# GroupNorm on one core: an inner loop of four quarters, with register addresses, for VectorE's scaling

## Chip, cores, metric

One core of a Trainium2 (trn2) chip. The metric is device time in microseconds (us), the median of several executions. "Span" is the time from the first to the last instruction in the profile, a little under the device time.

## The reference

```python
def reference(x, g, b):            # x: 128 x 1024 x 32 x 16, bfloat16; 32 groups
    xr = x.reshape(B, G, C // G, H, W)
    mu = xr.mean(axis=(2, 3, 4), keepdims=True)
    var = ((xr - mu) ** 2).mean(axis=(2, 3, 4), keepdims=True)
    xn = (xr - mu) / jnp.sqrt(var + 1e-5)
    return xn.reshape(B, C, H, W) * g[None, :, None, None] + b[None, :, None, None]
```

The input is 134 MB and so is the output. Each must cross between HBM and SBUF once.

## The kernel before

The work is cut into 32 tiles of 4.19 MB (128 partitions x 16384 elements). Six slots of SBUF hold them, and a tile is scaled in place. For each tile, PE sums, VectorE makes the negative mean from the sum, ScalarE squares and sums (in two halves) and makes the standard deviation, and VectorE makes 32 pairs of scale and shift and applies them to 32 pieces of 512 columns.

SyncE issues all loads and stores, in this order. Note that loads 6 and 7 stand behind store 1 in its program, and load 6 can start only when store 0 has landed:

```python
for j in range(SLOTS):             # SLOTS = 6
    load(j)
for i in range(NT):                # NT = 32
    store(i)                       # waits for 4 increments of s_done per tile
    if i % RUN == RUN - 1:         # RUN = 2: stores in pairs, then loads in pairs
        first = i + 1 + SLOTS - RUN
        for j in range(first, min(first + RUN, NT)):
            load(j)                # waits until the slot's store has landed
```

VectorE, the engine that the change touches:

```python
def on_vector(e):
    e.addr_align(256, offset=128, max_nops=0)
    # ... memsets, the first mean ...
    with nc.Fori(0, NT, 1, engines=[e.engine]) as i:
        # ... mean of tile i+1; wait for ScalarE's result of tile i;
        #     reciprocal, scl (32 scales), bia (32 shifts), each with a drain ...
        for k in range(KC):                      # KC = 32, unrolled
            a = ring[:, bass.ds((i % SLOTS) * F + k * HW, HW)]
            e.tensor_scalar(
                out=a, in0=a, scalar1=scl[:, k : k + 1], scalar2=bia[:, k : k + 1],
                op0=ALU.mult, op1=ALU.add,
            )
            if k % (KC // NQ) == KC // NQ - 1:   # NQ = 4
                e.drain()
                e.sem_inc(s_done, 1)
```

Of the kernel before, what the change touches and what calls it, by code (L numbers as in the profile page):

```python
# [8 lines left out]
ALU = mybir.AluOpType  # L9
# [7 lines left out]
SLOTS = 6  # L17
# [3 lines left out]
NQ = 4  # L21
# [4 lines left out]
def kernel(  # L26
# [12 lines left out]
    nc = tc.nc  # L39
# [3 lines left out]
    HW = H * W  # L43
# [4 lines left out]
    KC = C // G  # L48
    F = KC * HW
# [9 lines left out]
    def sbuf(name, shape, dtype):  # L59
        return nc.alloc_sbuf_tensor(name, shape, dtype)  # L60


    ring = sbuf("ring", [P, SLOTS * F], BF16)
# [14 lines left out]
    scl = sbuf("scl", [P, KC], F32)  # L78
    bia = sbuf("bia", [P, KC], F32)
# [3 lines left out]
    def sem(name):  # L83
        return nc.alloc_semaphore(name)
# [6 lines left out]
    s_gbp, s_sum, s_mean, s_rstd, s_done = (  # L91
        sem("gbp"), sem("sum"), sem("mean"), sem("rstd"), sem("done"),
    )
# [110 lines left out]
                ).then_inc(s_rstd, 1)  # L204

    def on_vector(e):
        e.addr_align(256, offset=128, max_nops=0)
        e.memset(ones_b[:], 1.0)  # L208
        e.memset(eps_t[:], EPS)
        e.drain()  # L210
        e.sem_inc(s_ones, 1)
        e.wait_ge(s_gbp, 1)
        e.tensor_copy(out=gb[:], in_=gb_p[:])  # L213

        def mean(ps_i, nm_i):
            e.tensor_scalar(  # L216
                out=jd[:], in0=ps_i, scalar1=-inv_n, scalar2=None,
                op0=ALU.mult, op1=ALU.add, accum_out=nm_i,
            ).then_inc(s_mean, 1)

        e.wait_ge(s_sum, 1)
        mean(ps[:, 0:MM_FREE], nm[:, 0:1])
        e.drain()
        with nc.Fori(0, NT, 1, engines=[e.engine]) as i:
            e.wait_ge(s_sum, i + 2)
            mean(
                ps[:, bass.ds(((i + 1) % 2) * MM_FREE, MM_FREE)],
                nm[:, bass.ds((i + 1) % 2, 1)],
            )
            e.wait_ge(s_rstd, i + 1)  # L230
            e.drain()  # L231
            e.reciprocal(out=inv[:], in_=rstd[:, bass.ds(i % 2, 1)])  # L232
            e.drain()
            e.tensor_scalar(  # L234
                out=scl[:], in0=gb[:, 0:KC], scalar1=inv[:], scalar2=None, op0=ALU.mult
            )
            e.drain()
            e.scalar_tensor_tensor(  # L238
                out=bia[:], in0=scl[:], scalar=nm[:, bass.ds(i % 2, 1)],
                in1=gb[:, KC : 2 * KC], op0=ALU.mult, op1=ALU.add,  # L240
            )
            e.drain()
            for k in range(KC):
                a = ring[:, bass.ds((i % SLOTS) * F + k * HW, HW)]
                e.tensor_scalar(  # L245
                    out=a, in0=a, scalar1=scl[:, k : k + 1], scalar2=bia[:, k : k + 1],
                    op0=ALU.mult, op1=ALU.add,
                )
                if k % (KC // NQ) == KC // NQ - 1:
                    e.drain()  # L250
                    e.sem_inc(s_done, 1)

    with tc.tile_critical(no_gpsimd_drain=True):  # L253
        on_sync(nc.sync)
        on_gpsimd(nc.gpsimd)
        on_tensor(nc.tensor)
        on_scalar(nc.scalar)
        on_vector(nc.vector)
# [30 lines left out]
```

## Time and profile before

| | before |
|---|---|
| device time, median (range) of 3 | 636.95 us (636.89 to 637.66) |
| span of the profiled run | 635.3 us |
| load and store queue, share of 16 DMA engines | 98.7% |
| ScalarE busy | 481.1 us (76%) |
| VectorE busy | 386.8 us (61%) |

The DMA queue line of the page (queue, kind: packets, MB, share of the 16 engines' span), and one line of its costliest groups (line, engine, operation, count, then busy us, mean ns of one, then idle time before and what ended it):

```profile
q1 hardware_dynamic: 10368, 268.44, 98.7%
...
L245 DVE TENSOR_SCALAR ring<-ring,scl,bia x1024 | 342.3, 408 | 28.2 <-issue 28.2
```

The DMA engines are full. Nothing else is above 76%.

The timeline of VectorE for one tile of the opening, before (start, duration, engine, line, operation, count, idle time before):

```profile
53.08 0.69 DVE L216 TENSOR_SCALAR_CACHE_REDUCE jd<-ps 128x512 bf16 x1 [0.77 <-issue]
...
55.10 0.16 DVE L232 RECIPROCAL inv<-rstd 128x1 f32 x1 [1.32 <-ACT rstd L201]
...
56.22 2.68 DVE L245 TENSOR_SCALAR ring<-ring,scl,bia  x8 [0.23 <-issue]
59.11 2.67 DVE L245 TENSOR_SCALAR ring<-ring,scl,bia  x8 [0.21 <-issue]
62.00 2.67 DVE L245 TENSOR_SCALAR ring<-ring,scl,bia  x8 [0.21 <-issue]
64.89 2.67 DVE L245 TENSOR_SCALAR ring<-ring,scl,bia  x8 [0.21 <-issue]
68.31 0.69 DVE L216 TENSOR_SCALAR_CACHE_REDUCE jd<-ps 128x512 bf16 x1 [0.75 <-issue]
```

A scaling shows 408 ns, but eight of them take 2.67 us: one starts every 0.323 us, overlapping its neighbour. Between quarters 0.21 us pass (drain, one register instruction, dispatch).

The timeline of SyncE's DMA issues before (a row with x2 merges two issues, and its second column runs from the start of the first to the end of the second):

```profile
52.37 15.59 SPq L123 DMA_DIRECT2D out_dram<-ring  x2
73.54 10.05 SPq L115 DMA_DIRECT2D ring<-in_x_dram  x2
83.64 15.02 SPq L123 DMA_DIRECT2D out_dram<-ring  x2
...
240.88 0.91 SPq L123 DMA_DIRECT2D out_dram<-ring  x2
269.99 10.11 SPq L115 DMA_DIRECT2D ring<-in_x_dram  x2
280.14 0.91 SPq L123 DMA_DIRECT2D out_dram<-ring  x2
```

Two regimes are to be seen. In the opening (first three rows) the two stores of a pair lie 15 us apart: SyncE waits for VectorE, which ScalarE paces. Later the pair goes out in 0.91 us: both tiles were ready, SyncE waits only for landings, and VectorE has slack.

The table of windows for the same stretch before (window, length, busy us of PE, PEld, DVE, ACT, POOL, granted clock, DMA share, GB/s):

```profile
68.00:76.00 8.00, 6.55 (x23) 2.73 (x24) 5.45 (x18) 7.86 (x5) 0.00 (x0) 0.70 0.94 406
76.00:84.00 8.00, 2.15 (x10) 0.78 (x8) 6.82 (x21) 7.85 (x3) 0.00 (x0) 0.94 1.04 451
84.00:92.00 8.00, 0.00 (x0) 0.00 (x0) 6.00 (x20) 7.71 (x5) 0.00 (x0) 0.50 0.96 414
92.00:100.00 8.00, 6.70 (x24) 2.81 (x25) 6.53 (x20) 7.85 (x3) 0.00 (x0) 0.71 1.04 442
```

The last column: the view counts a packet whole in the window in which it starts. So the DMA share can pass 1, and one packet of 32 KB more or less on each of the 16 engines changes an 8 us window by 65 GB/s. With the queue never empty the column stays at 406 to 451 GB/s. With each packet's bytes spread over its own time, worked out from the trace, it is 431 to 433 GB/s in all four windows.

### The profile page before, as it was taken

Reading aid. Unit: us, or ns where it says so; the run is one execution under the profiler, and the core shown is the slowest. Engines: PE = TensorE matmul, PEld = TensorE weight load, DVE = VectorE, ACT = ScalarE, POOL = GpSimd, SP = SyncE. Lnnn points to the kernel's source line nnn. Section 1 sums busy time; section 2 is a strip of 40 time slices with the busy share of each in tenths; the row PEclk is TensorE's granted clock in tenths of the full one; section 3 lists DMA queues with packets and bytes.
Section 4 is the critical chain, followed back from the end, with each engine's and each line's share of the span. In section 5 each row is a group of like instructions: output and inputs, shape, how many; then the busy total and the mean of one; then the engine's idle time right before and its main releaser. Section 6 shows DMA issues by size and latency. Waiting matters only on the chain.

```text
span 635.3 us, 6588 instructions
## 1 busy us (share of the span) xinstructions
PE 254.8 (40%) x1025; PEld 107.0 (17%) x1025; DVE 386.8 (61%) x1189; ACT 481.1 (76%) x194; POOL 0.8 (0%) x6
## 2 busy tenths in 40 slices
PE   1976518054180632707327072360823608163000
PEld 0332203021030210303113031120301203021000
DVE  0047777777757276572766727567275772757760
ACT  0499999999979498593986939779397793979800
POOL 0000000000000000000000000000000000000000
PEclk9999769568595685957859577595775958778555
DMA  8999999999999999999999999999999999999994
GB/s 362 429 437 421 429 431 427 435 433 435 435 429 429 429 429 437 431 439 435 429 429 429 429 435 431 431 429 427 423 433 421 437 427 419 427 427 431 429 416 205
DMA packets 10466, 268.46 MB, mean 423 GB/s; under 512 B 1248, under 2 KB 1248, under 8 KB 1248
## 3 DMA queue, kind: packets, MB, share of 16 engines
q1 hardware_dynamic: 10368, 268.44, 98.7%
q10 hardware_dynamic: 96, 0.00, 0.0%
q14 instruction: 2, 0.02, 0.0%
HBM read 134.22 MB, written 134.22 MB: 423 GB/s over the span
## 4 chain that ended last, share of the span: by engine, by line
DMA 51%; ACT 28%; PE 9%; DVEq 3%; DVE 3%; issue 2%; ACTq 1%; SPq 0%; POOLq 0%
DMA out_dram<-ring 34%; ACT ja L187 27%; DMA ring<-in_x_dram 17%; PE ps L165 9%; DVE ring L245 2%; DVEq L250 2%; DVEq L245 1%; ACT var L197 1%; DVEq L231 0%; ACTq L196 0%; ACT rstd L201 0%; ACTq L187 0%; DVE bia L238 0%; DVE scl L234 0%; DVE jd L216 0%
## 5 line engine op out<-in xcount | busy, mean ns | idle before, releaser
L187 ACT ACTIVATE ja<-ring,nm 128x8192 fp8e5 x64 | 455.8, 7122 | 113.7 <-DVE jd L216 108.2
L165 PE MATMUL ps<-ring,eye 128*128 x1024 | 254.6, 412 | 311.9 <-POOLq L154 300.2
L245 DVE TENSOR_SCALAR ring<-ring,scl,bia x1024 | 342.3, 408 | 28.2 <-issue 28.2
L165 PEld LDWEIGHTS ps<-ring,eye 128*128 128x128 bf16 x1024 | 106.9, 104 | 459.2 <-issue 363.4
L216 DVE TENSOR_SCALAR_CACHE_REDUCE jd<-ps 128x512 bf16 (+1 forms) x33 | 22.8, 692 | 139.4 <-PE ps L165 124.3
L232 DVE RECIPROCAL inv<-rstd 128x1 f32 x32 | 5.2, 164 | 40.2 <-ACT rstd L201 37.6
L187 ACT ACTIVATION_READ_ACCUMULATOR ja<-ring,nm 128x1 f32 x64 | 11.9, 186 | 0.0
L197 ACT ACTIVATE var<-sq,eps_t 128x1 f32<-128x1 f32 x32 | 9.4, 294 | 2.2
L201 ACT ACTIVATE rstd<-sq,var 128x1 f32<-128x1 f32 x32 | 9.4, 294 | 2.2
L238 DVE SCALAR_TENSOR_TENSOR bia<-scl,nm,gb 128x32 f32<-128x32 f32 x32 | 8.1, 252 | 4.7
L234 DVE TENSOR_SCALAR scl<-gb,inv 128x32 f32<-128x32 f32 x32 | 7.7, 242 | 2.7
L213 DVE COPY gb<-gb_p 128x64 f32<-128x64 f32 x1 | 0.2, 225 | 10.2 <-PE gb_p L159 10.2
L159 PE MATMUL gb_p<-gb_b,rep 32*128 32x64 bf16 x1 | 0.2, 208 | 11.8 <-DMA gb_b<-in_b_dram 11.8
L216 DVE DVE_READ_ACCUMULATOR jd<-ps (+1 forms) x33 | 2.7, 83 | 0.0
L181 ACT ACT_TABLE_LOAD x1 | 1.3, 1283 | 1.9 <-issue 1.9
L159 PEld LDWEIGHTS gb_p<-gb_b,rep 32*128 32x128 bf16 x1 | 0.1, 98 | 11.7 <-issue 11.7
L208 DVE MEMSET ones_b<- 128x128 bf16 x1 | 0.2, 165 | 1.7 <-SPq L253 1.7
L144 POOL TENSOR_SCALAR_AFFINE_SELECT rep<-ones_b 32x128 bf16<-32x128 bf16 x1 | 0.3, 303 | 0.0
L140 POOL TENSOR_SCALAR_AFFINE_SELECT eye<-ones_b 128x128 bf16<-128x128 bf16 x1 | 0.3, 292 | 1.4 <-DVEq L210 1.4
L181 ACT ACTIVATE warm<-eps_t 128x1 f32<-128x1 f32 x1 | 0.2, 202 | 0.0
L273 POOL MEMSET const-bfloat16-1.0<- 128x1 bf16 x1 | 0.1, 101 | 0.0
L273 POOL MEMSET const-uint8-127<- 128x1 uint8 x1 | 0.1, 101 | 0.0
(3 smaller groups left out, 0.3 us busy)
## 6 DMA issues: line engine op xcount, KB each, us to landing
ring<-in_x_dram SPq DMA_DIRECT2D x30, 4096.0 KB, 19.5
out_dram<-ring SPq DMA_DIRECT2D x30, 4096.0 KB, 29.2
ring<-in_x_dram SPq DMA_DIRECT2D x4, 2048.0 KB, 17.0
out_dram<-ring SPq DMA_DIRECT2D x8, 1024.0 KB, 20.2
gb_b<-in_g_dram ACTq DMA_DIRECT2D x1, 2.0 KB, 7.0
gb_b<-in_b_dram ACTq DMA_DIRECT2D x1, 2.0 KB, 10.2
```

Source lines behind the costliest of these rows:

```text
L159: e.matmul(out=gb_p[:], lhsT=rep[:], rhs=gb_b[:], start=True, stop=True).then_inc(s_gbp, 1)
L165: last = e.matmul(out=ps[:, bass.ds((i % 2) * MM_FREE, MM_FREE)], lhsT=eye[:], rhs=ring[:, bass.ds((i % SLOTS) * F + k * MM_FREE, MM_FREE) ...
L181: e.activation(out=warm[:], in_=eps_t[:], func=ACT.Sqrt)
L187: e.activation(out=ja[:], in_=ring[:, bass.ds((i % SLOTS) * F + h * (F // 2), F // 2)], func=ACT.Square, bias=nm[:, par : par + 1], scale=1.0,
L197: e.activation(out=var[:], in_=sq[:, 0:1], func=ACT.Identity, bias=eps_t[:], scale=inv_n)
L201: e.activation(out=rstd[:, par : par + 1], in_=sq[:, 1:2], func=ACT.Sqrt, bias=var[:], scale=inv_n,).then_inc(s_rstd, 1)
L216: e.tensor_scalar(out=jd[:], in0=ps_i, scalar1=-inv_n, scalar2=None, op0=ALU.mult, op1=ALU.add, accum_out=nm_i,).then_inc(s_mean, 1)
L232: e.reciprocal(out=inv[:], in_=rstd[:, bass.ds(i % 2, 1)])
L234: e.tensor_scalar(out=scl[:], in0=gb[:, 0:KC], scalar1=inv[:], scalar2=None, op0=ALU.mult)
L238: e.scalar_tensor_tensor(out=bia[:], in0=scl[:], scalar=nm[:, bass.ds(i % 2, 1)], in1=gb[:, KC : 2 * KC], op0=ALU.mult, op1=ALU.add,)
L245: e.tensor_scalar(out=a, in0=a, scalar1=scl[:, k : k + 1], scalar2=bia[:, k : k + 1], op0=ALU.mult, op1=ALU.add,)
L250: e.drain()
```

## The change

Intent: make VectorE's loop so short that all of its program lies in the first block of instructions (in these traces instructions arrive in packets of 8 KB), so that no alignment is needed. A loop over quarters holds eight scalings; since the quarter is a register, the addresses of scale and shift must come from registers too.

```diff
     def on_vector(e):
-        e.addr_align(256, offset=128, max_nops=0)
 ...
-            for k in range(KC):
-                a = ring[:, bass.ds((i % SLOTS) * F + k * HW, HW)]
-                e.tensor_scalar(
-                    out=a, in0=a, scalar1=scl[:, k : k + 1], scalar2=bia[:, k : k + 1],
-                    op0=ALU.mult, op1=ALU.add,
-                )
-                if k % (KC // NQ) == KC // NQ - 1:
-                    e.drain()
-                    e.sem_inc(s_done, 1)
+            with nc.Fori(0, NQ, 1, engines=[e.engine]) as q:
+                for k in range(KC // NQ):
+                    c = q * (KC // NQ) + k
+                    a = ring[:, bass.ds((i % SLOTS) * F + c * HW, HW)]
+                    e.tensor_scalar(
+                        out=a, in0=a, scalar1=scl[:, bass.ds(c, 1)], scalar2=bia[:, bass.ds(c, 1)],
+                        op0=ALU.mult, op1=ALU.add,
+                    )
+                e.drain()
+                e.sem_inc(s_done, 1)
```

## The prediction

> **What bounds the kernel now.** The DMA engines. The page's DMA queue table gives the load/store queue 98.7% of the 16 engines' span, and the table of windows shows 420 to 450 GB/s in nearly every 10 us up to 626 us. Each tile costs 2 x 4.19 MB, 19.7 us. VectorE has slack: 386.8 us busy (61%). In the timeline one tile costs it about 14.3 us, of which four quarters of 2.67 us. In the steady state the second tile of a pair is finished at 313.0 us and SyncE issues its store at 319.5 us: 6.5 us of slack. The chain of waits names ScalarE (28%) and PE, but mostly in the shadow of a full DMA queue.
>
> **What the change does.**
> 1. It removes the alignment instruction. Today VectorE branches at 1.04 us and its first memset starts at 1.66 us; now near 1.1 us. Worth nothing: the first matmul over data waits for a load that lands at 14.1 us.
> 2. Each of the 1024 scalings (L245) gets two fused register instructions instead of one. The scalings follow each other every 0.323 us, while the sequencer, where it runs ahead, takes 0.130 us for each. I estimate 0.24 to 0.28 us with the second instruction and the longer first one (today's register instructions take 0.05 to 0.15 us), still under 0.323 us. So a quarter keeps its 2.67 us.
> 3. Each quarter's head becomes serial: increment 0.04, branch 0.056, restart about 0.14 (today's outer back edge shows these), register instructions 0.15 and 0.06, gaps. I estimate 0.7 us idle before a quarter instead of 0.21: +2.0 us per tile, 14.3 becoming 16.3 us. The Trainium skill (Runtime: NRT & Kernel Launch, instruction fetch mechanics) says that a taken branch to a target outside the two held pages stalls for a fetch. The new body is small, so I expect none; no run here shows one yet.
>
> **On the critical path.** In the steady state nothing: +2 us per tile fits in 6.5 us. Only the opening is tight. The six first loads and store 0 are 29.4 MB; by 68 us the trace has moved all but 1.1 MB, about 2.5 us of work, and store 1 is issued at 67.6 us. Tiles 0 and 1 together delay it by about 3 us, to 70.5 us, when the queue is nearly dry; load 6 waits for store 0. That leaves a hole of 1 to 2.5 us, which a saturated queue never recovers. Later stores of the opening slip by 4 to 6 us, but with 5 to 11 MB queued. The last store is issued at 613.8 us with a queue lasting to 626 us; 2 to 4 us later is covered.
>
> **Predicted time:** 638.5 us, 80% range 636.4 to 641.5. Faster by over 2%: 0.01; within 2%: 0.95; slower by over 2%: 0.04.
>
> **What would show it.** Step 2: scalings still 0.32 us apart, busy time near 342 us. Step 3: idle before the scalings rising from 28.2 us to 85 to 95 us, 128 inner branches, no more instruction packets. Opening: store 1 near 70.5 us and a dip in DMA between 69 and 73 us. Steady state: stores in pairs, 39.3 us apart, never waiting for VectorE.
>
> **What would make it wrong.** A sequencer cost above 0.323 us per scaling (register pointers dearer than estimated): several us per tile; beyond about 6 us the stores slip. A code layout in which the inner branch fetches each time: 128 stalls, clearly slower. If the queue still holds work at 70.5 us, the change is exactly nothing, 637 us.

## More of the kernel before

A tile that waits for nothing takes 14.15 us from mean to mean. In the opening it takes 15.2 to 15.5 us, because VectorE waits for ScalarE's result (1.32 us in the second row shown): there ScalarE sets the pace.

## The result, and the profile after

| | before | after |
|---|---|---|
| device time, median (range) of 4 | 637.3 us (636.89 to 637.66) | 640.83 us (639.44 to 641.19) |
| span of the profiled run | 635.3 us | 639.1 us |
| VectorE's tile, nothing waited for | 14.15 us | 16.58 us |

The ratio is 1.0052 (95% interval 1.0034 to 1.0069): within 2%, but clear of noise, and slower.

The same lines of the page, after:

```profile
q1 hardware_dynamic: 10368, 268.44, 98.5%
...
L246 DVE TENSOR_SCALAR ring<-ring,scl,bia x1024 | 351.0, 413 | 91.5 <-issue 91.5
```

The first memset comes 0.55 us earlier, for nothing. The idle time ahead of the scalings has grown by 63 us, of which none is put down to another engine: "issue" means that the profile shows nothing else to wait for, and the records put VectorE's own sequencer (the part that reads its instructions and computes addresses) at work there.

VectorE's timeline, the same tile after:

```profile
55.79 0.69 DVE L215 TENSOR_SCALAR_CACHE_REDUCE jd<-ps 128x512 bf16 x1 [0.91 <-issue]
...
56.74 0.16 DVE L231 RECIPROCAL inv<-rstd 128x1 f32 x1 [0.24 <-issue]
...
58.17 2.75 DVE L246 TENSOR_SCALAR ring<-ring,scl,bia  x8 [0.53 <-issue]
61.70 2.74 DVE L246 TENSOR_SCALAR ring<-ring,scl,bia  x8 [0.77 <-issue]
65.21 2.74 DVE L246 TENSOR_SCALAR ring<-ring,scl,bia  x8 [0.77 <-issue]
68.72 2.74 DVE L246 TENSOR_SCALAR ring<-ring,scl,bia  x8 [0.78 <-issue]
72.37 0.69 DVE L215 TENSOR_SCALAR_CACHE_REDUCE jd<-ps 128x512 bf16 x1 [0.91 <-issue]
```

A quarter's start is 0.77 us after the end of the one before (0.21 us before the change), and a quarter itself takes 2.74 instead of 2.67 us. Where the second number comes from is in the view of one source line, its register instructions first before, then after (duration ns min/median/max):

```profile
L245 DVEq FUSED_REGOPS  x1024: 57/57/123, 40.8 to 611.9; - x171
```
```profile
L246 DVEq FUSED_REGOPS  x1920: 46/75/179, 41.4 to 622.1; - x192
```

In the sequence of records a scaling is now preceded by one of 179 ns and one of 46 ns, and with dispatch and gaps the sequencer needs 0.332 us, just more than the 0.323 us of the engine. The engine now follows the sequencer.

SyncE's issues after, the rows that answer to those of before:

```profile
54.94 16.93 SPq L123 DMA_DIRECT2D out_dram<-ring  x2
72.37 11.60 SPq L115 DMA_DIRECT2D ring<-in_x_dram  x2
88.09 16.92 SPq L123 DMA_DIRECT2D out_dram<-ring  x2
...
243.12 0.91 SPq L123 DMA_DIRECT2D out_dram<-ring  x2
272.29 10.22 SPq L115 DMA_DIRECT2D ring<-in_x_dram  x2
282.56 0.91 SPq L123 DMA_DIRECT2D out_dram<-ring  x2
```

Store 0 goes out 2.6 us later than before, store 1 at 71.5 instead of 67.6 us, store 2 at 88.1 instead of 83.6 us. Later, pairs still go out in 0.91 us. And the windows after:

```profile
68.00:76.00 8.00, 2.49 (x6) 0.96 (x7) 5.35 (x17) 6.59 (x5) 0.00 (x0) 0.67 0.82 352
76.00:84.00 8.00, 6.56 (x27) 2.64 (x25) 6.46 (x20) 7.85 (x3) 0.00 (x0) 0.90 1.05 393
84.00:92.00 8.00, 0.00 (x0) 0.00 (x0) 5.30 (x17) 6.59 (x5) 0.00 (x0) 0.74 1.06 459
92.00:100.00 8.00, 6.09 (x19) 2.45 (x20) 6.46 (x20) 7.85 (x3) 0.00 (x0) 0.62 0.91 393
```

In these 32 us the DMA moves 12.8 MB instead of 13.7 MB (rates times 8 us). With the bytes spread over each packet's own time the four rates are 384, 378, 427 and 433 GB/s, so it is mainly the first two windows that lose, and they differ in kind. In the first, the 16 engines stand idle for 0.8 us in all: when store 1 is issued, 0.04 MB is left in the queue. In the second no engine is idle and about 4 MB or more are queued, but from 80 to 84 us packets of 32 KB that otherwise take 1.21 us take up to 2.3 us. The same happens from 100 to 104 us. Longer packets cost 1.6 us between 76 and 110 us, against 0.2 us before. Why they take longer no run shows.

Summing the packets of both traces in order of completion, the changed kernel is level with before to within 0.3 us at seven tiles' worth of data (72 us; a tile is 4.19 MB), and then late by 1.3 us at eight, 1.9 us at ten, and 2.7 us at sixteen (160 us). It falls no further behind until 470 us. By the end it is 3.7 us late. So most is lost in the opening, and the rest, about 1 us, after 470 us.

### The profile page after: what moved, and what is told of

It is laid out like the page before. It is cut to its first block, busy times and chain, and to the rows that moved or that the text cites. A ratio compares the mean times of both kernels' runs of the same rounds, so it can differ in the third digit from the quotient of the medians.

```text
span 639.1 us, 7899 instructions
## 1 busy us (share of the span) xinstructions
PE 263.2 (41%) x1025; PEld 109.3 (17%) x1025; DVE 395.5 (62%) x1189; ACT 482.1 (75%) x194; POOL 0.8 (0%) x6
## 4 chain that ended last, share of the span: by engine, by line
DMA 53%; DVE 18%; issue 10%; DVEq 9%; PE 4%; ACT 2%; SPq 1%; ACTq 0%; POOLq 0%
DMA out_dram<-ring 45%; DVE ring L246 16%; DMA ring<-in_x_dram 7%; PE ps L165 4%; DVEq L246 4%; DVEq L242 3%; ACT ja L187 2%; DVEq L230 1%; DVE bia L237 1%; DVE scl L233 1%; DVEq L215 0%; DVE inv L231 0%; DVE jd L215 0%; SPq L115 0%; DVEq L223 0%
## 5 line engine op out<-in xcount | busy, mean ns | idle before, releaser
L246 DVE TENSOR_SCALAR ring<-ring,scl,bia x1024 | 351.0, 413 | 91.5 <-issue 91.5
L165 PE MATMUL ps<-ring,eye 128*128 x1024 | 263.0, 422 | 307.7 <-POOLq L154 288.8
L165 PEld LDWEIGHTS ps<-ring,eye 128*128 128x128 bf16 x1024 | 109.2, 107 | 461.2 <-issue 369.9
L215 DVE TENSOR_SCALAR_CACHE_REDUCE jd<-ps 128x512 bf16 (+1 forms) x33 | 22.8, 692 | 100.5 <-PE ps L165 81.4
L215 DVE DVE_READ_ACCUMULATOR jd<-ps (+1 forms) x33 | 2.7, 83 | 0.0
```

The lines of the kernel that those rows point to most:

```text
L165: last = e.matmul(out=ps[:, bass.ds((i % 2) * MM_FREE, MM_FREE)], lhsT=eye[:], rhs=ring[:, bass.ds((i % SLOTS) * F + k * MM_FREE, MM_FREE) ...
L215: e.tensor_scalar(out=jd[:], in0=ps_i, scalar1=-inv_n, scalar2=None, op0=ALU.mult, op1=ALU.add, accum_out=nm_i,).then_inc(s_mean, 1)
L246: e.tensor_scalar(out=a, in0=a, scalar1=scl[:, bass.ds(c, 1)], scalar2=bia[:, bass.ds(c, 1)], op0=ALU.mult, op1=ALU.add,)
```

## The experiments

Theory A: VectorE's longer tile matters only in the opening, where it delays stores 1 and 2 until the queue has nothing left. Rivals: B, the place of the code in the instruction blocks; C, an equal loss for every looped tile; D, the slower VectorE, or its register traffic, slows the DMA or the chain in some other way; E, the loop costs something besides its time.

### 1 and 2: the alignment alone

```diff
 # e1_no_align, against the kernel before; e2_loop_align is the changed kernel with this line added
-        e.addr_align(256, offset=128, max_nops=0)
```

> The kernel before without its alignment instruction, nothing else. Theory A (the time is lost in the opening, because slower scaling delays stores 1 and 2 until the DMA queue runs dry): 637.3 us, within 0.5 us of before, since the scaling is untouched. Rival B (code layout: what matters is where the loop lies in the instruction blocks): clearly slower, with more instruction packets than the 2 of before, and a longer head of each tile on VectorE.

> The changed kernel with the alignment instruction put back. Theory A: 640.8 us as the changed kernel, within 0.7 us; first memset back at 1.66 us. Rival B (the loss of the alignment costs the 3.5 us): 637.3 us.

Measured on the same chip (before: 637.05 us): e1 637.13 us, ratio 1.0002 (0.9988 to 1.0015); e2 640.49 us, ratio 1.0057 (1.0043 to 1.0070). e1 has 2 instruction packets, like before. Rival B is out for the bulk of the loss: the line is worth nothing either way. Something small does hang on it. In the five runs of e2 the device time is 1.69 to 1.75 us above the span, as in before; in the four of the changed kernel it is 2.09 to 2.14 us. Some 0.4 us of the changed kernel's time therefore lies outside the span, and in its trace an instruction packet stands at 640.99 us, after the span has ended. The only other kernel with both signs is e7 below, which has the same VectorE program. That this packet is the cause is likely, not shown.

### 3 and 4: which tiles

```diff
-        with nc.Fori(0, NT, 1, engines=[e.engine]) as i:
+        for first, last, trips in [(0, 8, 0), (8, 32, 4)]:   # e3; e4: [(0, 8, 4), (8, 32, 0)]
+            with nc.Fori(first, last, 1, engines=[e.engine]) as i:
+                tile_of(i, trips)      # trips 0: the unrolled code of before
```

Both start with an alignment of their own (offset 16), meant to put both loops in one block. The traces do not quite bear that out: e3 has an instruction packet at 169 us and e4 one at 185 us, near the change of loops. The data of e3 are no later after it than before it.

> Tiles 0 to 7 scaled by the unrolled code of before, tiles 8 to 31 by the inner loop, both loops in one aligned block. Theory A: 637.3 to 638.0 us, no hole in the DMA between 70 and 90 us, although VectorE takes 16.6 us for each of 24 tiles. Rival C (every looped tile costs the same, wherever it stands, 3.5 us / 32): 639.9 us.

> The mirror: tiles 0 to 7 by the inner loop, tiles 8 to 31 unrolled. Theory A: 639.3 to 640.8 us, with the same two holes in the DMA near 71 and 84 us. Rival C: 638.2 us.

Measured (before: 637.05 us): e3 638.03 us, ratio 1.0020 (1.0006 to 1.0033); e4 640.32 us, ratio 1.0051 (1.0037 to 1.0064). The windows of e3:

```profile
68.00:76.00 8.00, 5.66 (x18) 2.31 (x19) 5.01 (x17) 7.86 (x5) 0.00 (x0) 0.61 0.96 414
76.00:84.00 8.00, 3.33 (x16) 1.30 (x14) 7.49 (x23) 7.85 (x3) 0.00 (x0) 1.00 1.06 459
```

No hole: 414 and 459 GB/s where the changed kernel had 352 and 393. Eight looped tiles at the beginning cost 3.3 us, 24 elsewhere cost 1.0 us. Rival C expected the opposite order. But e3 is slightly above Theory A's range, and its interval excludes zero: the looped tiles of the steady state are not free.

In e3 a looped tile took 17.48 us, not 16.58: the same inner branch was followed by about 0.25 us until the next instruction instead of 0.135 us. The only known difference is the place of the loop in the block. Even so e3 lost only 1.0 us.

### 5 and 6: the first three tiles

The same edit with `[(0, 3, 4), (3, 32, 0)]` for e5 and `[(0, 3, 0), (3, 32, 4)]` for e6.

> Inner loop for tiles 0 to 2 alone, the other 29 unrolled. Theory A (two holes, behind stores 0 and 1, because stores 1 and 2 come late): 638.6 to 640.3 us, with the loss already made by 90 us. Rival C (a share per looped tile): 637.4 us.

> The mirror: tiles 0 to 2 unrolled, 29 tiles by the inner loop. Theory A: 637.0 to 638.3 us, stores 1 and 2 issued near 68 and 84 us as before. Rival C: 640.2 us.

Measured (before on this chip: 636.57 us): e5 638.94 us, ratio 1.0031 (1.0019 to 1.0043); e6 637.93 us, ratio 1.0018 (1.0005 to 1.0031). Three looped tiles of 32 cost 2.4 us, the other 29 cost 1.4 us. The ratios less one add up (0.0031 + 0.0018 = 0.0049) to nearly the 0.0052 and 0.0057 of all tiles looped. In e5 the packets were 1.9 us late at eight tiles' worth of data and 3.4 us late at eleven (111 us, not by 90 us as expected). Then they no longer fell behind, and were 2.0 us late at the end; in e6 they were level to within 0.3 us until 314 us.

### 7 and 8: early stores, VectorE unchanged

```diff
     def store_parts(i):
-        return NQ if i >= NT - IN_PARTS else 1
+        return NQ if i >= NT - IN_PARTS or i < 3 else 1
 ...
-                e.wait_ge(st[j % SLOTS], 16 * (j // SLOTS))
+                e.wait_ge(st[j % SLOTS], 16 * sum(store_parts(t) for t in range(j % SLOTS, j, SLOTS)))
```

e7 is the changed kernel with this edit, e8 the kernel before with it.

> The changed kernel, all tiles by the inner loop, but the stores of tiles 0 to 2 in four parts, each issued when its quarter is scaled, so that the queue has work when the first loads end. Theory A: 636.5 to 638.0 us, the two holes gone though VectorE is as slow as in the changed kernel. Rival D (the slower VectorE itself, or its register traffic, slows the DMA or the chain): 640.8 us, no gain.

> The kernel before with the same early stores in parts. Theory A: the queue of before hardly ran dry, so at most 0.5 us of gain: 636.5 to 637.3 us.

Measured (before: 636.57 us): e7 639.67 us, ratio 1.0050 (1.0037 to 1.0063); e8 638.00 us, ratio 1.0021 (1.0008 to 1.0034). Both miss their ranges. Taken by the time alone, e7 speaks for rival D. The windows of e7 say otherwise:

```profile
68.00:76.00 8.00, 2.56 (x7) 0.97 (x8) 5.41 (x17) 6.59 (x5) 0.00 (x0) 0.64 1.01 425
76.00:84.00 8.00, 6.31 (x27) 2.58 (x25) 6.45 (x20) 7.85 (x3) 0.00 (x0) 0.93 1.05 448
84.00:92.00 8.00, 0.00 (x0) 0.00 (x0) 5.30 (x18) 6.59 (x5) 0.00 (x0) 0.71 1.02 438
92.00:100.00 8.00, 7.33 (x23) 2.94 (x24) 6.46 (x21) 7.85 (x3) 0.00 (x0) 0.65 1.03 442
```

The holes are gone although VectorE is just as slow (at ten tiles' worth of data e7 is level with before), and longer packets cost only 0.4 us between 76 and 110 us. What e7 gained there it paid elsewhere: its data are within 0.8 us of before until 350 us, those of e8 within 0.6 us, and both lose the rest after that. The control e8 shows that the early stores in parts themselves cost 1.4 us on a kernel whose queue had no hole; why was not found. By spans, medians of the runs: before 634.9, e8 636.3, e7 637.5 us. So with early stores the loop costs 1.2 us of span, the same size as the rest that e3 and e6 left (1.0 and 1.3 us by spans), and on top e7 has the 0.4 us outside the span. The sum fits; it is a sum made after the fact.

### 9: time without a loop

```diff
             for k in range(KC):
+                if k % (KC // NQ) == 0:
+                    for _ in range(3 if k < KC // 2 else 2):
+                        e.reciprocal(out=pad[:], in_=inv[:])   # 128 x 1, result unused
+                        e.drain()
```

Here `pad` is a new tile of 128 x 1, and the alignment is at offset 16.

> The unrolled kernel before, with ten tiny drained reciprocals per tile (three, three, two, two, ahead of its quarters) that stretch VectorE's tile from 14.15 to about 16.6 us, the time of a looped tile; no inner branch, no register addresses for scale and shift. Theory A (only VectorE's time per tile matters): 640.0 to 641.3 us, stores 1 and 2 near 71 and 88 us. Rival E (the inner loop itself costs something besides its time): below 639 us. In the steady state the second store of a pair should land on the last engine 9.88 us after the first, as with looped tiles, if time is all that matters, and 9.82 us, as before, if not.

Measured (before: 636.98 us): 641.96 us, ratio 1.0069 (1.0055 to 1.0083). The tile took 16.77 us, stores 1 and 2 went out at 73.3 and 90.1 us, and the scalings were those of before (408 ns each). No inner branch, no register address of scale or shift, and the loss is there, larger with a still later store 1. The windows:

```profile
68.00:76.00 8.00, 1.13 (x5) 0.41 (x4) 6.16 (x21) 6.38 (x5) 0.00 (x0) 0.70 0.72 307
76.00:84.00 8.00, 8.00 (x27) 3.04 (x25) 6.75 (x25) 7.85 (x3) 0.00 (x0) 0.66 1.00 393
```

A bare delay is enough: the engines stand idle for 2.5 us, and longer packets cost another 1.9 us by 110 us. So neither register traffic (rival D) nor the loop itself (rival E) is needed for the opening's loss, and in e7 both were present without it. The time lies 0.7 us above the expected range, with stores 1 and 2 about 2 us later than expected.

### 10, 11 and 12: the number of heads

```diff
-            with nc.Fori(0, NQ, 1, engines=[e.engine]) as q:
-                for k in range(KC // NQ):
-                    c = q * (KC // NQ) + k
+            per = KC // trips                       # trips 1, 2 or 8
+            with nc.Fori(0, trips, 1, engines=[e.engine]) as q:
+                for k in range(per):
+                    c = q * per + k
 ...
-                e.drain()
-                e.sem_inc(s_done, 1)
+                    if (k + 1) % min(per, KC // NQ) == 0:
+                        e.drain()
+                        e.sem_inc(s_done, 1)
```

With eight trips SyncE counts eighths. One and two trips have an alignment at offset 16.

> One trip of 32 scalings: register addresses for all, one loop head per tile instead of four. Tile about 15.4 us (16.6 less three heads of 0.4 us each). Theory A: 637.8 to 639.3 us, between before and the changed kernel, store 1 near 69.5 us. If the register addresses and not the heads made the loss: 640 us and more.

> Eight trips of four scalings, eight heads per tile: about 20.0 us per tile, more than the 19.7 us that the DMA engines need. VectorE becomes the bound: 40 us before the first scaling, 32 tiles of 20.0 us, and about 12 us for the last stores: 680 to 697 us, stores waiting for VectorE to the end. If the opening alone counted, whatever the tile time: 645 us.

> Two trips of sixteen scalings, addresses of scale and shift from registers as in the changed kernel (with one trip they had been folded into constants), two loop heads per tile instead of four. Tile about 15.8 us: 32 scalings at 0.332 us, two heads of 0.78 us, two drains inside a trip at about 0.39 us. Theory A: stores 1 and 2 near 70 and 86 us, and 638.2 to 640.0 us, between before and the changed kernel. If heads do not matter and register addresses alone do: 640.5 us and more. In the steady state the second store of a pair should land 9.88 us behind the first on the last engine if register addresses cause that, 9.82 to 9.85 us if the four heads do.

| kernel | trips | tile, us | store 1 issued, us | store 2 issued, us | median, us | ratio to before (95%) | MB queued at store 1 | engines idle between 70 and 80 us | lost to longer packets between 76 and 110 us |
|---|---|---|---|---|---|---|---|---|---|
| e10_trips1 | 1 | 14.38 | 68.2 | 84.4 | 637.28 | 1.0003 (0.9990 to 1.0017) | 1.53 | 0.0 us | 0.1 us |
| e12_trips2 | 2 | 15.87 | 70.3 | 86.2 | 638.94 | 1.0035 (1.0021 to 1.0048) | 0.63 | 0.0 us | 1.5 us |
| changed kernel | 4 | 16.58 | 71.5 | 88.1 | 640.83 | 1.0052 (1.0034 to 1.0069) | 0.04 | 0.8 us | 1.6 us |
| e9_delay_all | none | 16.77 | 73.3 | 90.1 | 641.96 | 1.0069 (1.0055 to 1.0083) | 0.03 | 2.5 us | 1.9 us |
| e11_trips8 | 8 | 19.99 | 77.4 | 97.4 | 684.99 | 1.0756 (1.0739 to 1.0772) | 0.00 | 6.9 us | 1.9 us |

e10 came out below its range, for a reason that the built program shows: with one trip the loop variable is known to be zero, so the addresses of scale and shift were folded back into constants and the scalings stayed at 408 ns. It tests one loop head, not register addresses, and one head is free: its tile of 14.38 us is still shorter than the 15.2 to 15.5 us that ScalarE allows in the opening. e12 does have register addresses (413 ns), and lies between, as Theory A expected. In these five the time rises with the moment of stores 1 and 2.

The last three columns, worked out from one trace of each kernel, correct Theory A on one point. In e12 the queue never ran dry and no engine stood idle, and yet its data were 1.6 us late at ten tiles' worth: all of it went into packets that took longer. e2 is the same (0.40 MB queued, no idle time, 1.8 us). e4 and e5 had 0.06 and 0.05 MB queued, 1.3 us of idle time and 1.8 us of longer packets. Where 1.2 MB or more were queued at store 1 (before 1.70, e1 2.07, e3 1.39, e6 1.24, e10 1.53) there was no idle time and at most 0.2 us of longer packets. So late stores cost time in two ways, and an empty queue is only one of them.

e11 shows the other end. VectorE's timeline there:

```profile
313.81 1.41 DVE L258 TENSOR_SCALAR ring<-ring,scl,bia  x4 [0.78 <-issue]
315.99 1.41 DVE L258 TENSOR_SCALAR ring<-ring,scl,bia  x4 [0.78 <-issue]
318.31 0.69 DVE L215 TENSOR_SCALAR_CACHE_REDUCE jd<-ps 128x512 bf16 x1 [0.91 <-issue]
```

Every 2.19 us a head of 0.78 us; no wait for another engine is left. The tile of 19.99 us exceeds the DMA's 19.7 us, VectorE bounds the kernel, and 48 us are lost. The step from 16.6 to 20.0 us costs more than ten times what the step from 14.15 to 16.6 us costs: that is where the slack ends.

### What stays open

Why packets take longer after late stores. And a rest of 1.0 to 1.4 us for looped tiles after the opening (e3, e6). SyncE's pairs of stores give a hint. Between 320 and 440 us a pair follows the last after 39.30 to 39.33 us in before, e4 and e5 (steady state unrolled), and after 39.38 to 39.45 us in the changed kernel, e2, e3, e6, e7 and e12 (steady state looped).

The expectations of e9 and e12 had set a test for its cause: how long after the first store of a pair the second one lands. In that stretch it is 9.81 to 9.83 us in before. e9, with long tiles and constant addresses, has 9.84 to 9.87 us (pairs 39.33 to 39.35 us apart), nearer to before. e12, with register addresses and two heads, has 9.88 to 9.90 us, like the changed kernel's 9.86 to 9.92 us. By that measure the register addresses make the difference, and neither the tile's time nor the number of heads. It is one trace each, and e1 and e8, with before's scalings, reach 39.38 and 39.40 us between pairs.

Nor is the difference the loss itself: the data of e3 and e6 are within 0.4 us of before until 350 us. They fall behind only after 400 us, where longer packets cost every kernel but e11 between 2.0 and 3.7 us up to 610 us, looped (3.5 in e3) or not (3.4 in e8). What makes the rest stays open.

## Why the prediction was right or wrong

The time (640.83 us, predicted 638.5, range 636.4 to 641.5) and the class (within 2%) were right, and so was the main mechanism: late stores in the opening. The range was wide, and part of the agreement is luck: of the loss, the engines' idle time, which the prediction counted on, is 0.8 us, and the rest comes from things that it did not have. Point by point:

- **DMA bound, VectorE with slack**: right. e11 is beyond the slack's end: its tile of 19.99 us is more than the DMA's 19.7 us.
- **Step 1, alignment worth nothing**: right within the span (e1: ratio 1.0002). The 0.4 us outside the span was not foreseen.
- **Step 2, "still under 0.323 us. So a quarter keeps its 2.67 us"**: wrong. The term for the sequencer was mis-sized: 0.24 to 0.28 us estimated, 0.332 us measured, because the first of the two register instructions takes 179 ns. It crossed the limit by 3%, so it cost only 0.07 us per quarter, and busy time became 351.0 instead of 342 us.
- **Step 3, heads**: the idle time before the scalings was predicted at 85 to 95 us and is 91.5 us. The tile was mis-sized: +2.0 us predicted, 2.43 us measured. The Trainium skill (Runtime: NRT & Kernel Launch, instruction fetch mechanics) warns of a fetch stall at a taken branch whose target is outside the two held pages; here the trace shows no such stall. The 96 inner branches that go back cost 0.056 us plus 0.135 us each, and no 8 KB instruction packet arrives between the start and 638 us.
- **"That leaves a hole of 1 to 2.5 us"**: right in kind, mis-sized. Store 1 came 3.9 us later, not 3, but the hole was 0.8 us of idle time in the profiled run. The data were 2.7 us late by 160 us because packets also took longer at 80 to 84 and 100 to 104 us (1.6 us), which the prediction did not have. Later stores did slip "with 5 to 11 MB queued" (6.3 MB at store 2). What is false is that with work still queued "the change is exactly nothing": e12 had 0.63 MB queued at store 1 and no idle time, and lost 1.7 us. Nor is such a loss always final: e5 was 3.4 us late at 111 us and 2.0 us at the end.
- **"In the steady state nothing"**: wrong by 1.0 to 1.4 us (e3, e6). SyncE's pairs still go out in 0.91 us there, as predicted, and still something is lost, after 400 us. This is the step that failed; its cause is open.

## What to carry to other kernels

When the DMA queue bounds a kernel, a slower engine is free only as long as its results are ready well before the queue runs out of work (here 1.2 MB queued was enough, 0.63 MB was not); look for the moments when the queue is thinnest, above all where the first loads end and the first stores must take over. A short loop with computed addresses has two costs to add up: a serial head after each drain (0.57 us more per quarter here), and register arithmetic per instruction, which is free only while the sequencer stays faster than the engine. Look at packets one by one before you call a dip in a table of windows a hole: a DMA engine can be busy all the time and move less. And a remedy needs its own control: the early stores filled the hole, and most of the gain was lost elsewhere.

## What the Trainium skill lacked or had wrong

- No page that I found gives the cost of register arithmetic on VectorE's sequencer. Here (operations counted in the built program) a fused register instruction of three operations took 57 ns, and one of six took 179 ns in the scaling loop but 146 ns at L215, so the count alone does not set it. It would belong in Advanced Engine Details and Errata, beside its control flow timing.
- Advanced Engine Details and Errata (control flow timing) gives about 108 ns for compare-and-branch. The trace shows 56 ns for the instruction plus 135 ns until the next one of the loop starts. With the loop at another place in the block (e3) the latter was about 0.25 us; the page has nothing on place.
- Runtime: NRT & Kernel Launch (instruction fetch mechanics) describes the fetch at a branch. It says nothing of an instruction packet that arrives after the last instruction: in the changed kernel and e7 one did, and 0.4 us more of device time lay outside the span. That the one causes the other is not shown.
- DMA: Bandwidth & Descriptors: no figure was found there for what it costs to split a store of 4.19 MB on a full queue. The kernel with three stores in four parts each, instead of whole, took 1.4 us longer (e8), though its data were at most 0.6 us late until 350 us.
